# Gate groups with two tokens across the partitions, made three steps ahead, in an FNet plus PEER kernel

## The chip, the cores and the metric

The kernel runs on one core of a Trainium2 chip. The metric is the device time of one execution in microseconds. Times of one version are given as the median of several runs; the profile is one execution with the hardware profiler.

## The reference

```python
def _A_ref(x, ...):                       # FNet: real part of a 2-D Fourier transform
    a = einsum("bsd,ed->bse", x, dft_hid_re); b = einsum("bsd,ed->bse", x, dft_hid_im)
    return einsum("ts,bse->bte", dft_seq_re, a) - einsum("ts,bse->bte", dft_seq_im, b)

def _B_ref(x, w_q, k1, k2, u, v):         # PEER: 4096 experts of one neuron, S=2048, D=512, H=32, E=64
    q = einsum("nd,dhc->nhc", xf, w_q); q1, q2 = q[..., :128], q[..., 128:]
    s1 = einsum("nhd,ed->nhe", q1, k1); s2 = einsum("nhd,ed->nhe", q2, k2)
    # the two best of s1 and of s2, the two best of their four sums: expert = i1 * 64 + i2
    g = softmax(top_s)                                    # two gates for each token and head
    act = gelu(einsum("nd,nhkd->nhk", xf, u[top_e]))
    return einsum("nhk,nhk,nhkd->nd", g, act, v[top_e])

xn = layernorm(x)
return x + _A_ref(xn, ...) + _B_ref(xn, ...)
```

The Fourier matrices are inputs, and the kernel uses their symmetries, so it also checks on the chip that they have them.

## The kernel before, in words

The program has three stages. The first, to about 50 us, computes the Fourier half, with folded matrices. The second, to about 443 us, computes the scores of 16 blocks of 128 tokens for eight groups of heads, finds the best two with VectorE, and leaves for each token 64 pairs (two experts of 32 heads) of expert number and gate. The third, the expert stage, is where the change lies. (A second copy of the program for inputs without these symmetries stands behind it and is not run.)

**The expert stage, block by block.** Fourteen blocks of 128 tokens go through all 4096 experts with dense matmuls; the last two blocks (256 tokens) are done by gathering rows instead. For a block `b`:

- `u_part(b, cg)`, eight steps: products of the block's input `xb` with 4 of the 32 expert columns (48 products of 128 columns, L959), then GELU on ScalarE (L962) into `act`.
- Gates: a dense table of gates, 128 x 32 experts for each token, is itself made by matmuls. `compact` transposes a block's pairs, so that the 128 partitions hold a token's 64 pairs twice: once with the f16 high part of the gate, once with the rest. `g_mm(b, tg)` makes the table of 32 tokens: for every token a tile `L` (partition by 128: is this the expert's lower number?) and a tile `R` (partition by 32: is this its upper number?, times the gate) come from comparisons on VectorE, L983 in two halves of 16 tokens, L991 and L994, and one product of L and R gives the token's 128 x 32 gates in PSUM (L996, 32 columns). A block has four such groups. They go into two PSUM tiles `pg` of two banks in turn.
- `w_part(b, tg)`: VectorE multiplies the group's gates by the activations in place (L1007), ScalarE takes the f16 high half (L1012), VectorE subtracts it for the low half (L1015). The last subtraction frees the PSUM tile.
- `v_part(b, pv, cg)`, eight steps: 12 products of 512 columns each with `v` (L1024), accumulated; `finish` adds and stores (L1039).

**The order.** The main loop runs, for b from 0 to 13, eight steps of `v_part(b)` and then eight steps of `u_part(b + 2)`. Dictionaries say at which step a group is made (`vg`, `ug`) and at which it is used (`vw`, `uw`). Before, a group of block b + 1 was made in v steps 3 and 7 and in u steps 3 and 7, and used in v steps 0 and 4 and u steps 0 and 4. For the last block the groups 2 and 3 were made at v steps 2 and 4 and all four used at v steps 0, 2, 4, 6. Within an engine, a scheduler sets the order of instructions; every engine works through its queue in order.

**Between the steps** other work is spread. `pick` takes one piece of the gathered tokens' work for each step: `fetch` (an indirect DMA of a row of u and v into one of `BUFS` = 6 buffers `ga`), `dot` on VectorE (L1066), `gain` on ScalarE (L1076 to L1079) and an addition on GpSimd (L1084), which then issues the next fetch. `paced` takes the checks: `compare` (a slice of the Fourier matrices, L755, L761), `compare_r` (rows, L1129 to L1135), `compare_w` (the wide matrices, L1153 to L1174) and `fit`. Each loads into one of three buffers with the tag `w` through SP's queue, which also carries `xb` (L942), `zb` (a block's pairs) and `y`. `after(k, f)` puts `f` k steps later. At the end `verdict` reduces the checks with two reductions over partitions on GpSimd (L1210, L1212) and makes the `flags` (L1231) on which the program branches.

Of the kernel before, what the change touches and what calls it, by code (L numbers as in the profile page):

```python
# [36 lines left out]
def tile_fnet_peer(ctx, tc, x, ca, cb, c5, wt, wf, wr, wq, kt, ut, vn, uv, out):  # L37
# [14 lines left out]
    z_d = dram.tile([NT, P, 3 * P], F16, name="z_d")  # L52
# [503 lines left out]
    def part_b(safe, stS, stP, stE, xt, u_sb, cmp_p):  # L556
# [55 lines left out]
        z = sp.tile([P, NT, 3, 2, 2, H], F16, name="z")  # L612
# [17 lines left out]
        def routing(part, j, vals, idx, t0=0, t1=NT, ge=nc.gpsimd):  # L630
# [20 lines left out]
            elif part == 1:  # L651
# [5 lines left out]
                nc.vector.tensor_copy(zi[:, :, 2, :, 0, hs], g)  # L657
                if not safe and t1 == NT:
                    nc.gpsimd.tensor_copy(gts[:, :, :, hs], g[:, n - NS:])
                nc.vector.tensor_tensor(zi[:, :, 2, :, 1, hs], g, zi[:, :, 2, :, 0, hs], op=ALU.subtract)  # L660
            else:
# [25 lines left out]
                for l in range(2):  # L687
                    for w, v in enumerate((lc, e)):
                        ge.tensor_copy(zi[:, :, w, :, l, hs], v)
# [3 lines left out]
        def compact(b, src, pool, tag):  # L693

            cmp = pool.tile([P, 3, P, 2], F16, tag=tag, name=f"cmp{b}")
# [3 lines left out]
            nc.scalar.activation(cmp, p[:, :3 * P].rearrange("p (w n) -> p w n", w=3).unsqueeze(3)  # L699
                                 .to_broadcast([P, 3, P, 2]), AF.Copy)  # L700
            CMP[b] = cmp
# [163 lines left out]
        for j in range(NCH):  # L865
# [8 lines left out]
            for i in range(NT):  # L874
                spare, mm = scores(j, i, vals, idx)
                for f in () if safe else checks.get(j * NT + i, ()):
                    f(mm)
                for t, f in ((j * NT + i, y_rows), (j * NT + i - 10, y_store)):
                    if t in HID and not safe:
                        f(HID[t])  # L880
                if j == 1 and not safe:
                    nc.sync.dma_start(xt_d[i], xt[i].rearrange("p a k n -> p (a k n)"))
                mst = MST if j else MST0
                if j + 1 < NCH and i in mst:
                    m_stage(j + 1, wq_tile, mst[i])
                if j == 0 and i == 10 and not safe:
                    sums()
                if j + 2 < NCH and i == 9:
                    m_stage(j + 2, wq_tile, 0)
                if i in (1, 2, 4) and pend is not None:  # L890
                    routing((0, 2, None, 1)[i - 1], *pend)
                if j + 1 == NCH and i == 4:
                    for part in range(3):
                        routing(part, j, vals, idx, 0, 4, nc.vector)
                if j + 1 == NCH and i == NT - 1:
                    for b in range(2):
                        compact(b, z[:, b].rearrange("p w k t h -> p w (k t h)"), cmp_p, f"cmp{b}")
                    nc.sync.dma_start(z_d[2:4].rearrange("i p f -> p i f"),
                                      z[:, 2:4].rearrange("p i a k t h -> p i (a k t h)"))
# [8 lines left out]
        nc.sync.dma_start(z_d[4:].rearrange("i p f -> p i f"),  # L908
                          z[:, 4:].rearrange("p i a k t h -> p i (a k t h)"))
# [7 lines left out]
        RS = [lr.tile([P, 32, NC], F16, name=f"R{k}") for k in range(2)]  # L917
# [16 lines left out]
        BUFS = 6  # L934
# [10 lines left out]
        def compact_d(b):  # L945
            zb = bp.tile([P, 3, P], F16, tag="zb", name=f"zb{b}", bufs=1)
# [27 lines left out]
        def g_mm(b, tg, after=None):  # L974
            cmp = CMP[b]
            p = pg(f"g{b}_{tg}")
            def bc(w, t0, t1, n):
                return cmp[:, w, tg * TG + t0:tg * TG + t1, :].unsqueeze(2).to_broadcast([P, t1 - t0, n // 2, 2])

            for hf in range(2):  # L980
                LS.append(LS.pop(0))
                L = LS[-1]
                nc.vector.tensor_tensor(  # L983
                    L.rearrange("p t (l two) -> p t l two", two=2),
                    io_lam.rearrange("p (l two) -> p l two", two=2).unsqueeze(1).to_broadcast([P, 16, P // 2, 2]),
                    bc(0, hf * 16, hf * 16 + 16, P), op=ALU.is_equal)
                if hf == 0:
                    RS.append(RS.pop(0))
                    R = RS[-1]
                    Rv = R.rearrange("p t (c two) -> p t c two", two=2)  # L990
                    nc.vector.tensor_tensor(  # L991
                        Rv, io_c.rearrange("p (c two) -> p c two", two=2).unsqueeze(1)
                        .to_broadcast([P, TG, NC // 2, 2]), bc(1, 0, TG, NC), op=ALU.is_equal)
                    nc.vector.tensor_tensor(Rv, Rv, bc(2, 0, TG, NC), op=ALU.mult)  # L994
                for t in range(16):
                    i = nc.tensor.matmul(p[:, hf, t * NC:(t + 1) * NC], L[:, t, :], R[:, hf * 16 + t, :],  # L996
                                         start=True, stop=True)
                    if after is not None:
                        follow(i.ins, after)
# [109 lines left out]
        def compare_r(n):  # L1109
# [14 lines left out]
            def work():  # L1124
                for ri, odd, e in cls:
                    sgn = (((1, 1, 1), (-1, 1, -1)), ((-1, -1, 1), (1, -1, -1)))[ri][odd]
                    f = (-1 if ri else 1) * sgn[1] * sgn[2]
                    m = ALU.add if ri else ALU.subtract
                    nc.vector.tensor_tensor(tv[e, 1], tv[e, 1], tv[e, 0], op=ALU.subtract if sgn[0] > 0 else ALU.add)  # L1129
                    nc.vector.tensor_tensor(tv[e, 3], tv[e, 3], tv[e, 2], op=ALU.subtract if f > 0 else ALU.add)  # L1130
                    nc.vector.tensor_tensor(t[e, 0::2, 2:4], t[e, 0::2, 2:4], t[e, 0::2, 0:2], op=m)
                    if odd and ri:
                        nc.vector.tensor_copy(t[e, 2, 0:2], t[e, 0, 0:2])
                    elif odd == ri:
                        nc.vector.memset(t[e, 2, 0:2], 0.0)  # L1135
                after(2, lambda: nc.scalar.activation(tf[:, P:], tf[:, P:], AF.Abs, accum_out=chk[:, n:n + 1]))

            after(2, work)

        def compare_w(n):  # L1140
# [7 lines left out]
            if half:  # L1148
# [4 lines left out]
            nc.vector.tensor_reduce(asum[:, n:n + 1], v[0], axis=AX.X, op=ALU.add, apply_absolute_value=True)  # L1153
            nc.vector.tensor_tensor(v[1][:, even], v[1][:, even], v[0][:, even], op=op)
            nc.vector.tensor_tensor(v[1][:, odd], v[1][:, odd], v[0][:, odd], op=po)
            nc.vector.tensor_tensor(v[3][0:1], v[3][0:1], v[2][0:1], op=op)
            nc.vector.scalar_tensor_tensor(v[3][:, even], v[0][:, even], not0, v[3][:, even],  # L1157
                                           op0=ALU.mult, op1=ALU.subtract)
            nc.vector.scalar_tensor_tensor(v[3][:, odd], v[0][:, odd], not0, v[3][:, odd],  # L1159
                                           op0=ALU.mult, op1=ALU.add)  # L1160

            r = v[2][0:1]
            a, m = (slice(0, P, 2), slice(P, 256, 2)) if ri else (slice(1, P - half, 2), slice(P + 1, 256 - half, 2))
            nc.vector.tensor_tensor(r[:, m], r[:, m], r[:, a], op=op)  # L1164
            nc.vector.memset(r[:, 1 - ri:P:2], 0.0)  # L1165
            if half and not ri:
                nc.vector.memset(r[:, 255:256], 0.0)
            nc.vector.scalar_tensor_tensor(v[2], v[0], not0, v[2], op0=ALU.mult, op1=op)  # L1168
            if ri:
                nc.scalar.activation(v[0][0:1, 0:P], v[0][0:1, 0:P], AF.Abs, accum_out=chk[0:1, 69 + half:70 + half])  # L1170
            c = P - half
            nc.vector.tensor_tensor(v[0][:, P:P + c], v[0][:, P:P + c], v[0][:, 0:c], op=op)  # L1172
            if half and not ri:
                nc.vector.memset(v[0][:, 255:256], 0.0)  # L1174
            f = t.rearrange("p k e -> p (k e)")[:, P - half * ri:]
            after(2, lambda: nc.scalar.activation(f, f, AF.Abs, accum_out=chk[:, n + 1:n + 2]))
# [60 lines left out]
        units.insert(2, lambda: compare_r(64))  # L1237
# [43 lines left out]
        for tg in range(2):  # L1281
            g_mm(1, tg)
# [8 lines left out]
        for b in range(NB):  # L1291
            pv = pc(f"v{b}")
            if b + 2 < NB:
                vw, vg, uw, ug = {0: 0, 4: 1}, {3: 2, 7: 3}, {0: 2, 4: 3}, {3: 0, 7: 1}
            else:
                vw, vg = {0: 0, 2: 1, 4: 2, 6: 3}, {2: 2, 4: 3}
            for cg in range(8):
# [27 lines left out]
                elif b:  # L1325
                    pick(mm, cg % 2)
# [7 lines left out]
            for cg in range(8 if b + 2 < NB else 0):  # L1334
# [6 lines left out]
                if cg in ug:  # L1341
                    g_mm(b + 2, ug[cg], mm)
# [150 lines left out]
```

## Time and profile before

| | |
|---|---|
| median of 3 runs | 1110.06 us (1107.38 to 1111.2) |
| profiled execution, its own time | 1110.31 us |
| its span | 1108.5 us |
| TensorE busy (PE) | 1070.5 us, 97% |
| VectorE busy (DVE) | 963.9 us, 87% |
| ScalarE busy (ACT) | 717.3 us, 65% |
| GpSimd busy (POOL) | 595.4 us, 54% |
| DMA | 178 GB/s mean |

In the rows that follow, a group reads: line, engine, operation, output <- inputs, shape, count | busy us, mean ns | idle us before, and what ended it. A row of the waits reads: engine and line <- engine and line waited for: us in total, times, longest. A row of the timeline starts with its time and its length in us.

### The profile page before, as it was taken

What the parts mean: (1) busy time and instruction counts of PE and PEld (TensorE: products, weight loads), DVE (VectorE), ACT (ScalarE), POOL (GpSimd) and SP (SyncE); (2) the same over time, 40 slices, a digit from 0 to 9 for tenths busy, and PEclk for the clock granted to TensorE, in tenths of its full rate; (3) what the DMA queues carried; (4) which work ended last, traced back from release to release, by engine and by line L of the source; (5) the groups of instructions that cost most, each with busy time, mean ns of one, the idle gap of its engine ahead of it and who ended that gap; (6) DMA issues with size and microseconds to landing.
All of it is one profiled execution on the core that took longest, in us unless ns stands there. A gap on an engine that the chain in (4) does not pass through costs nothing. (4 is left out here: it accounts for less than half of the span.)

```text
span 1108.5 us, 28483 instructions
## 1 busy us (share of the span) xinstructions
PE 1070.5 (97%) x11070; PEld 696.6 (63%) x11070; DVE 963.9 (87%) x2748; ACT 717.3 (65%) x1326; POOL 595.4 (54%) x553
## 2 busy tenths in 40 slices
PE   5899999999999999999989999999999999999987
PEld 4355555454544544987675967858667696776933
DVE  6879897979999999987999798999998889998971
ACT  3566657778788767533756766668666776767650
POOL 0013537588797846211646575665575656556431
PEclk9799999999999999999999999999999999999999
DMA  8248153435445331463568667766876667666511
GB/s 326 84 168 288 39 210 99 174 130 208 152 153 197 110 123 65 152 212 92 183 189 248 193 206 244 223 220 191 242 232 214 209 204 252 222 200 200 166 29 51
DMA packets 84936, 196.78 MB, mean 178 GB/s; under 512 B 10770, under 2 KB 27559, under 8 KB 84792
## 3 DMA queue, kind: packets, MB, share of 16 engines
q1 hardware_dynamic: 63898, 123.55, 33.0%
q0 software_dynamic: 20736, 71.31, 21.7%
q8 instruction: 88, 1.44, 0.5%
q14 instruction: 56, 0.46, 0.1%
q10 hardware_dynamic: 158, 0.01, 0.0%
HBM read 177.74 MB, written 17.10 MB: 176 GB/s over the span
## 5 line engine op out<-in xcount | busy, mean ns | idle before, releaser
L799 PE MATMUL s<-m,xq 128*128 128x512 f16 x1536 | 338.9, 379 | 0.0
L959 PE MATMUL z<-xb,u 128*128 128x128 f16 x5376 | 306.4, 220 | 0.0
L959 PEld LDWEIGHTS <-u 128*128 128x128 f16 x5376 | 302.1, 98 | 0.0
L1024 PE MATMUL v<-v,act 128*128 128x512 f16 x1344 | 300.2, 382 | 1.6 <-DVE act L1015 1.6
L1084 POOL TENSOR_TENSOR ov<-ov,ga 128x512 f32<-128x512 f32 x128 | 176.9, 1382 | 206.9 <-ACT ga L1079 173.4
L799 PEld LDWEIGHTS <-xq 128*128 128x128 f16 x1536 | 148.3, 98 | 171.3 <-issue 0.2
L1024 PEld LDWEIGHTS <-act 128*128 128x128 f16 x1344 | 129.6, 98 | 153.2 <-issue 4.5
L983 DVE TENSOR_TENSOR L<-io_lam,cmp 128x2048 f16<-128x2048 f16 x112 | 154.7, 1405 | 31.2 <-PE g L996 31.1
L1050 POOL DMA_INDIRECT ga<-in_uv_dram,eix x128 | 153.4, 1198 | 48.1 <-POOL ov L1084 36.9
L807 DVE MAX8 vals<-ss 128x8 f32<-128x64 f32 x1024 | 152.5, 216 | 14.0 <-ACT ss L804 14.0
L962 ACT ACTIVATE act<-z,scl 128x512 f32<-128x512 f32 x112 | 76.1, 681 | 93.6 <-PE z L959 92.9
L811 DVE FIND_INDEX8 idx<-vals,ss 128x8 uint16<-128x256 f32 x256 | 107.1, 419 | 0.0
L804 ACT ACTIVATE ss<-s,wsc 128x512 f32<-128x512 f32 x112 | 75.5, 680 | 43.1 <-PE s L799 33.8
L1079 ACT ACTIVATE ga<-ga,za 128x512 f32<-128x512 f32 x128 | 92.3, 722 | 10.2 <-ACT za L1077 0.4
L781 ACT ACTIVATE cx<-cx 128x896 f32<-128x896 f32 x64 | 60.6, 947 | 48.7 <-DVE cx L761 36.3
L1066 DVE SCALAR_TENSOR_TENSOR ga<-ga,px 128x512 f32<-128x512 f32 x128 | 85.7, 676 | 0.2
L1012 ACT ACTIVATE act<-g 128x1024 f16<-128x1024 f32 x56 | 73.2, 1308 | 18.2 <-DVE g L1007 18.2
L1007 DVE SCALAR_TENSOR_TENSOR g<-act,scl,g 128x1024 f32<-128x1024 f32 x56 | 71.6, 1279 | 10.7 <-ACT act L962 6.6
L1015 DVE TENSOR_TENSOR act<-g,act 128x1024 f16<-128x1024 f32 x56 | 72.7, 1298 | 6.6 <-ACT act L1012 6.5
L169 POOL TENSOR_TENSOR wq<-wq,wh 128x1024 f16<-128x1024 f32 x26 | 55.5, 2136 | 24.2 <-ACT wq L166 23.7
L996 PE MATMUL g<-R,L 128*128 128x32 f16 x1792 | 53.8, 176 | 13.0 <-DVE act L1015 12.5
L996 PEld LDWEIGHTS <-L 128*128 128x128 f16 x1792 | 51.6, 96 | 21.7 <-DVE act L1015 8.7
(281 smaller groups left out, 1298.4 us busy)
## 6 DMA issues: line engine op xcount, KB each, us to landing
cx<-in_cb_dram SPq DMA_DIRECT2D x50, 448.0 KB
wq<-in_wq_dram SPq DMA_DIRECT2D x32, 512.0 KB
fit<-in_wq_dram SPq DMA_DIRECT2D x28, 512.0 KB
uv<-in_ut_dram SPq DMA_DIRECT2D x16, 512.0 KB
uv<-in_vn_dram SPq DMA_DIRECT2D x16, 512.0 KB
cx<-in_cb_dram SPq DMA_DIRECT2D x28, 224.0 KB
xq<-in_x_dram SPq DMA_DIRECT2D x8, 512.0 KB
xt_d<-xq SPq DMA_DIRECT2D x16, 256.0 KB
```

The costliest lines, as they stand in the source:

```text
L799: mm = nc.tensor.matmul(ps, xt[i][:, l, kd, :], m[:, r, kd, :], start=(n == 0), stop=(n == 3 * KD - 1))
L807: nc.vector.max(vals[:, i, w, :, h], s[:, g, :])
L811: nc.vector.max_index(idx[:, i, w].rearrange("p k h -> p (k h)"), vals[:, i, w, 0:2].rearrange("p k h -> p (k h)"), s[:, w * HC:g + 1, :]. ...
L959: mm = nc.tensor.matmul(p[:, cc * P:(cc + 1) * P], ug[:, l, c % 2, kd, :], xb[:, r, kd, :], start=(n == 0), stop=(n == 3 * KD - 1))
L962: GL[mm.ins.name] = nc.scalar.activation(act[:, cg * 4:cg * 4 + 4, :].rearrange("p c n -> p (c n)"), p, AF.Gelu_apprx_tanh, scale=zsc)
L983: nc.vector.tensor_tensor(L.rearrange("p t (l two) -> p t l two", two=2), io_lam.rearrange("p (l two) -> p l two", two=2).unsqueeze(1).to_ ...
L996: i = nc.tensor.matmul(p[:, hf, t * NC:(t + 1) * NC], L[:, t, :], R[:, hf * 16 + t, :], start=True, stop=True)
L1024: mm = nc.tensor.matmul(pv, w16[:, c, :, l], vg[:, r, c % 2, :], start=(c == 0 and k == 0), stop=(c == NC - 1 and k == 2))
L1050: nc.gpsimd.indirect_dma_start(out=t, out_offset=None, in_=uv, in_offset=bass.IndirectOffsetOnAxis(ap=eix[:, n].rearrange("p k h -> p (k h ...
L1066: nc.vector.scalar_tensor_tensor(t, t, 1.0, T["x"], op0=ALU.mult, op1=ALU.mult, accum_out=T["z", n][:, s:s + 1])
L1079: nc.scalar.activation(t, t, AF.Copy, scale=z)
L1084: T["a"] = nc.gpsimd.tensor_tensor(o, o, t, op=ALU.add)
```

## The change

1. A token's list of 64 pairs now lies in half of the partitions, and two tokens share one tile: the even token in partitions 0 to 63, the odd one in 64 to 127. One `L` tile (16 pairs of tokens) serves a group of 32 tokens. `R` becomes two tiles, for the high and the low part of the gate, each with 64 columns: 32 for the even token, 32 for the odd, with zeros (cleared once by GpSimd) where a partition belongs to the other token. Each pair of tokens gets two accumulating products of 64 columns.
2. VectorE makes, for a group, one `L`, one `one_hot`, and four parts of `R` (high and low, even and odd; 64 partitions, 512 elements each). `compact` transposes four times instead of three and copies with three ScalarE instructions instead of one.
3. Groups are made at v steps 1 and 5 (groups 1 and 2 of block b + 1), u step 1 (group 3 of block b + 1) and u step 5 (group 0 of block b + 2). Uses stay where they were; in the last block the last use moves from step 6 to 5.
4. `BUFS` is 5 instead of 6.
5. The work of `compare_r` and `compare_w` is cut into pieces of one step each, and the four `compare_w`, which were last, are spread among the first checks. No pieces of the gathered tokens' work are picked in v steps of block 12.

The diff, cut to its core:

```diff
-        RS = [lr.tile([P, 32, NC], F16, name=f"R{k}") for k in range(2)]
+        RS = [lr.tile([P, 2, 16, 2, NC], F16, name=f"R{k}") for k in range(2)]
+        one_hot = lr.tile([P, 16, NC], F16, name="one_hot")
+        for R in RS:
+            nc.gpsimd.memset(R, 0.0)
-        BUFS = 6
+        BUFS = 5
...
-            for w in range(3):
-                nc.tensor.transpose(p[:, w * P:(w + 1) * P], src[:, w], ident16)
-            nc.scalar.activation(cmp, p[:, :3 * P].rearrange("p (w n) -> p w n", w=3).unsqueeze(3)
-                                 .to_broadcast([P, 3, P, 2]), AF.Copy)
+            for w in range(4):
+                nc.tensor.transpose(p[:, w * P:(w + 1) * P], src[:, w:w + 2].rearrange("p w s -> p (w s)"), ident16)
+            for a, w0, w1, o in ((0, 0, 4, 0), (1, 0, 3, 1), (1, 3, 4, -3)):
+                r = slice(64 * a, 64 * a + 64)
+                nc.scalar.activation(cmp[r, w0 + o:w1 + o], p.rearrange("p (w n a) -> p w a n", w=4, a=2)[r, w0:w1, a]
+                                     .unsqueeze(3).to_broadcast([64, w1 - w0, 64, 2]), AF.Copy)
...
-            for hf in range(2):
-                LS.append(LS.pop(0))
-                L = LS[-1]
-                nc.vector.tensor_tensor(
-                    L.rearrange("p t (l two) -> p t l two", two=2),
-                    io_lam.rearrange("p (l two) -> p l two", two=2).unsqueeze(1).to_broadcast([P, 16, P // 2, 2]),
-                    bc(0, hf * 16, hf * 16 + 16, P), op=ALU.is_equal)
...
-                for t in range(16):
-                    i = nc.tensor.matmul(p[:, hf, t * NC:(t + 1) * NC], L[:, t, :], R[:, hf * 16 + t, :],
-                                         start=True, stop=True)
+            nc.vector.tensor_tensor(
+                two(L), io_lam.rearrange("p (l two) -> p l two", two=2).unsqueeze(1).to_broadcast([P, 16, P // 2, 2]),
+                bc(0, P), op=ALU.is_equal)
+            nc.vector.tensor_tensor(
+                two(one_hot), io_c.rearrange("p (c two) -> p c two", two=2).unsqueeze(1)
+                .to_broadcast([P, 16, NC // 2, 2]), bc(1, NC), op=ALU.is_equal)
+            for l in range(2):
+                for a in range(2):
+                    r = slice(64 * a, 64 * a + 64)
+                    nc.vector.tensor_tensor(two(R[r, l, :, a]), two(one_hot[r]), bc(2 + l, NC, r), op=ALU.mult)
+            pv = p.rearrange("p h n -> p (h n)")
+            for t in range(16):
+                for l in range(2):
+                    i = nc.tensor.matmul(pv[:, t * 64:(t + 1) * 64], L[:, t, :],
+                                         R[:, l, t].rearrange("p a c -> p (a c)"), start=l == 0, stop=l == 1)
...
-            after(2, work)
+            for k, c in enumerate(cls):
+                after(3 + k, lambda c=c: work(*c))
+            after(8, lambda: nc.scalar.activation(tf[:, P:], tf[:, P:], AF.Abs, accum_out=chk[:, n:n + 1]))
...
-            after(2, lambda: nc.scalar.activation(f, f, AF.Abs, accum_out=chk[:, n + 1:n + 2]))
+            for k, part in enumerate((first, second, third, last)):
+                after(2 + k, part)
+            after(7, lambda: nc.scalar.activation(f, f, AF.Abs, accum_out=chk[:, n + 1:n + 2]))
...
-        units.insert(2, lambda: compare_r(64))
+        for n in range(4):
+            units.insert(3 + 6 * n, units.pop())
+        units.insert(6, lambda: compare_r(64))
...
-                vw, vg, uw, ug = {0: 0, 4: 1}, {3: 2, 7: 3}, {0: 2, 4: 3}, {3: 0, 7: 1}
+                vw, vg, uw, ug = {0: 0, 4: 1}, {1: 1, 5: 2}, {0: 2, 4: 3}, {1: (1, 3), 5: (2, 0)}
+                if b + 3 == NB:
+                    ug[7] = 2, 1
             else:
-                vw, vg = {0: 0, 2: 1, 4: 2, 6: 3}, {2: 2, 4: 3}
+                vw, vg = {0: 0, 2: 1, 4: 2, 5: 3}, {2: 2, 4: 3}
...
-                elif b:
-                    pick(mm, cg % 2)
...
-                    g_mm(b + 2, ug[cg], mm)
+                    g_mm(b + ug[cg][0], ug[cg][1], mm)
```

How the change moves VectorE's queue shows at the start of the v steps of block 1, where block 2's gates are used (`g_0`, `g_1` are its first two groups, `cmp` its lists, `act` its activations, `ga` gathered rows, `cx` a check; what an instruction waits for stands in brackets). Before:

```order
L1007 SCALAR_TENSOR_TENSOR g_0_7307<-act_6973,scl,g_0_7307 128x32x32 [waits Activation_49]
L761 TENSOR_TENSOR cx_7468<-cx_7468 128x128 [waits DVE_49]
L983 TENSOR_TENSOR L_5792<-io_lam,cmp_6977 128x2048 [waits PE_49]
L1066 SCALAR_TENSOR_TENSOR ga_6_7196,za_7117<-ga_6_7196,px_7116 128x512 [waits DMASW1_49,Pool_49]
L983 TENSOR_TENSOR L_5793<-io_lam,cmp_6977 128x2048 [waits PE_49]
L1007 SCALAR_TENSOR_TENSOR g_1_7583<-act_6973,scl,g_1_7583 128x32x32
L1066 SCALAR_TENSOR_TENSOR ga_7_7255,za_7117<-ga_7_7255,px_7116 128x512 [waits DMASW2_49,Pool_49]
L1015 TENSOR_TENSOR act_6973<-g_0_7307,act_6973 128x32x32 [waits Activation_49]
```

The changed kernel at the same place:

```order
L1015 SCALAR_TENSOR_TENSOR g_0_7446<-act_6948,scl,g_0_7446 128x32x32 [waits Activation_49]
L762 TENSOR_TENSOR cx_7487<-cx_7487 128x128 [waits DVE_49]
L1074 SCALAR_TENSOR_TENSOR ga_6_7272,za_7097<-ga_6_7272,px_7096 128x512 [waits DMASW1_49,Pool_49]
L1074 SCALAR_TENSOR_TENSOR ga_7_7392,za_7097<-ga_7_7392,px_7096 128x512 [waits DMASW2_49,Pool_49]
L1023 TENSOR_TENSOR act_6948<-g_0_7446,act_6948 128x32x32 [waits Activation_49]
L1015 SCALAR_TENSOR_TENSOR g_1_7647<-act_6948,scl,g_1_7647 128x32x32 [waits PE_49]
L991 TENSOR_TENSOR L_5790<-io_lam,cmp_6952 128x2048
L1000 TENSOR_TENSOR R_5792<-one_hot,cmp_6952 64x16x32 x4
```

The two L tiles and the second multiply have left the place between the first multiply and its subtraction (L1015 before, L1023 now), and the second multiply now waits for its products.

VectorE's queue at the start of the v steps of block 12, where block 13's gates are used. Before:

```order
L1007 SCALAR_TENSOR_TENSOR g_0_16064<-act_15714,scl,g_0_16064 128x32x32 [waits Activation_49]
L1157 SCALAR_TENSOR_TENSOR cx_16377<-cx_16377,not_87 128x128 [waits DVE_49]
L1159 SCALAR_TENSOR_TENSOR cx_16377<-cx_16377,not_87 128x128
L1164 TENSOR_TENSOR cx_16377<-cx_16377 1x64
L1007 SCALAR_TENSOR_TENSOR g_1_16340<-act_15714,scl,g_1_16340 128x32x32 [waits PE_49]
L1165 MEMSET cx_16377 1x64 [waits DVE_49]
L983 TENSOR_TENSOR L_5792<-io_lam,cmp_15718 128x2048
L1168 SCALAR_TENSOR_TENSOR cx_16377<-cx_16377,not_87 128x256 [waits DVE_49]
L1066 SCALAR_TENSOR_TENSOR ga_61_16011,za_11802<-ga_61_16011,px_11801 128x512 [waits DMASW3_49,Pool_49]
L983 TENSOR_TENSOR L_5793<-io_lam,cmp_15718 128x2048
L1172 TENSOR_TENSOR cx_16377<-cx_16377 128x127 [waits Activation_49]
L1015 TENSOR_TENSOR act_15714<-g_0_16064,act_15714 128x32x32
```

The changed kernel:

```order
L1015 SCALAR_TENSOR_TENSOR g_0_16332<-act_15830,scl,g_0_16332 128x32x32 [waits Activation_49]
L1015 SCALAR_TENSOR_TENSOR g_1_16488<-act_15830,scl,g_1_16488 128x32x32 [waits PE_49]
L991 TENSOR_TENSOR L_5790<-io_lam,cmp_15834 128x2048
L1000 TENSOR_TENSOR R_5792<-one_hot,cmp_15834 64x16x32 [waits DVE_49]
L1000 TENSOR_TENSOR R_5792<-one_hot,cmp_15834 64x16x32 x3
L756 TENSOR_TENSOR cx_16529<-cx_16529 128x256 [waits DMAHW7_49,DMAHW6_49]
L756 TENSOR_TENSOR cx_16529<-cx_16529 128x512
L1023 TENSOR_TENSOR act_15830<-g_0_16332,act_15830 128x32x32 [waits Activation_49]
```

The wide check and the gathered row are gone from between the first multiply and its subtraction; a plain check in two parts, one L and the four R parts stand there.

GpSimd's queue at the end (`ov` sums the gathered rows, `y` is the last block's input to its sum, L1210 and L1230 the reductions over partitions). Before:

```order
L1084 TENSOR_TENSOR ov_11920<-ov_11920,ga_61_16011 128x512 [waits DMASW3_49,Activation_49,Pool_49]
L1084 TENSOR_TENSOR ov_11920<-ov_11920,ga_62_16120 128x512 [waits DMASW4_49,Activation_49,Pool_49]
L1033 DMA y_16611<-in_x_dram 128x512 [waits DMAHW1_49,DMAHW0_49,DVE_49]
L1084 TENSOR_TENSOR ov_11920<-ov_11920,ga_63_16233 128x512 [waits DMASW5_49,Activation_49,Pool_49]
L1210 ISA
L1210 ISA fr<-fa 128x2
```

The changed kernel:

```order
L1041 DMA y_16744<-in_x_dram 128x512 [waits DMAHW1_49,DMAHW0_49,DVE_49]
L1092 TENSOR_TENSOR ov_11982<-ov_11982,ga_61_16225 128x512 [waits DMASW3_49,Activation_49,Pool_49]
L1092 TENSOR_TENSOR ov_11982<-ov_11982,ga_62_16379 128x512 [waits DMASW4_49,Activation_49,Pool_49]
L1092 TENSOR_TENSOR ov_11982<-ov_11982,ga_63_16436 128x512 [waits DMASW5_49,Activation_49,Pool_49]
L1230 ISA
L1230 ISA fr<-fa 128x2
```

Two more additions now stand behind the transfer of y.

More of the change, by code (lines that the diff above doesn't have):

```diff
@@ L1168, in compare_w, with first @@
[L1168 to L1174, printed above, removed]
+            r = v[2][0:1]
+            def first():
+                nc.vector.tensor_reduce(asum[:, n:n + 1], v[0], axis=AX.X, op=ALU.add, apply_absolute_value=True)
+                nc.vector.tensor_tensor(v[1][:, even], v[1][:, even], v[0][:, even], op=op)
+                nc.vector.tensor_tensor(v[1][:, odd], v[1][:, odd], v[0][:, odd], op=po)
@@ L1175, in compare_w, with last @@
+            def last():
+                if ri:
+                    nc.scalar.activation(v[0][0:1, 0:P], v[0][0:1, 0:P], AF.Abs,
+                                         accum_out=chk[0:1, 69 + half:70 + half])
+                c = P - half
+                nc.vector.tensor_tensor(v[0][:, P:P + c], v[0][:, P:P + c], v[0][:, 0:c], op=op)
+                if half and not ri:
+                    nc.vector.memset(v[0][:, 255:256], 0.0)
             f = t.rearrange("p k e -> p (k e)")[:, P - half * ri:]
-            after(2, lambda: nc.scalar.activation(f, f, AF.Abs, accum_out=chk[:, n + 1:n + 2]))
+            for k, part in enumerate((first, second, third, last)):
+                after(2 + k, part)
@@ L1280, in part_b @@
                 g_mm(0, cg // 2 + 2)
[L1281 to L1282 removed]
+        g_mm(1, 0)
         last = list(range(V2, 16)) if safe else []
```

92 lines of the change are left out of this document (44 added, 48 removed).

## Prediction

> **What bounds the kernel now.** I read the page first, then TensorE's own waits in the expert stage (from 443 us on), then the clock by stretches, and last the timeline around the long waits.
>
> ```profile
> span 1108.5 us, 28483 instructions
> 443.00:1081.00 638.00, 623.90 (x8461) 471.50 (x8458) 572.40 (x859) 410.26 (x851) 343.48 (x272) 0.99 0.64 196
> ```
>
> The second row is the expert stage: length, then busy time of PE, weight load, DVE, ACT and POOL, the granted clock, and DMA. TensorE is busy for 623.9 of 638 us, VectorE for 572.4. So a microsecond of matmul added here is a microsecond of the end, and what can be won is the little that TensorE waits, and what these waits do to its clock:
>
> ```profile
> PE g L996 <- DVE act L1015: 12.5, 8, 3.9
> PE v L1024 <- DVE act L1015: 1.6, 1, 1.6
> PE g L996 <- DVE L L983: 0.3, 1, 0.3
> 556.00:578.00 22.00, 18.91 (x308) 17.15 (x306) 21.22 (x30) 10.86 (x23) 9.64 (x9) 0.92 0.64 193
> 798.00:820.00 22.00, 20.32 (x383) 19.50 (x381) 20.48 (x26) 18.29 (x39) 14.26 (x12) 0.98 0.80 238
> 820.00:842.00 22.00, 22.00 (x128) 10.27 (x127) 19.12 (x28) 12.94 (x30) 10.98 (x10) 0.94 0.71 211
> 1062.00:1084.00 22.00, 18.72 (x135) 8.90 (x135) 13.75 (x19) 9.97 (x20) 6.02 (x5) 0.92 0.14 31
> ```
>
> The waits are 14.4 us (total, times, longest). Almost all have one cause: a gate group's products need a PSUM buffer, and there are two, so group k+2 waits until VectorE has subtracted (L1015) in the buffer of group k. After three of these waits the clock falls below 1.00: 22 us times 0.08 + 0.02 + 0.06 + 0.08 is 5.3 us lost. Together **19.7 us** hang on VectorE's lateness. Two places show what it is late with:
>
> ```profile
> 559.80 0.43 DVE L1129 TENSOR_TENSOR cx_r<-cx_r 4x256 f32<-4x256 f32 x1
> 561.93 0.97 PE L996 MATMUL g<-R,L 128*128 128x32 f16 x32 [3.10 <-DVE act L1015]
> ...
> 1051.18 8.58 PE L1024 MATMUL v<-v,act 128*128 128x512 f16 x39
> 1054.83 1.29 DVE L1007 SCALAR_TENSOR_TENSOR g<-act,scl,g 128x1024 f32<-128x1024 f32 x1 [2.67 <-ACT act L962]
> 1056.03 1.24 DVE L1157 SCALAR_TENSOR_TENSOR cx<-cx,not 128x128 f32<-128x128 f32 x1
> 1062.33 1.30 DVE L1015 TENSOR_TENSOR act<-g,act 128x1024 f16<-128x1024 f32 x1
> 1063.68 0.95 PE L996 MATMUL g<-R,L 128*128 128x32 f16 x32 [3.92 <-DVE act L1015]
> ```
>
> Both times a check (rows of cx) stands in VectorE's queue ahead of the subtraction that TensorE is waiting for.
>
> **What goes.** A group is now made three steps before VectorE uses it instead of five. A step is 12 products of 512 columns (39 take 8.58 us above), about 2.7 us. Its PSUM buffer was wanted three steps after the previous use and is wanted five steps after it: 5.4 us more room. The longest wait of the steady blocks is 3.1 us, so there all should go. The checks in pieces help the same way (nothing extra is counted for it). The wait of 1.6 us before the last block goes because its last group is taken a step earlier (2.7 us). Only group 2 of block 13 keeps its place: made at step 2, its buffer used at step 0. There VectorE now has, between the first multiply and its subtraction, a second multiply, a list tile L, four R parts and two check pieces. From the rows above and below: 1.3 + 1.3 + 1.2 + 4 x 0.42 + 1.6, then 1.3 for the subtraction, 8.4 us from the start of the multiply. TensorE comes for it after 36 products at 0.22 (8.58 / 39), 7.9 us after the block begins. The multiply waits for the last GELU and began 3.65 us after the block (1051.18 to 1054.83); at best it begins with it. Ahead of that GELU stood a check and two rows in ScalarE's queue, now one row, so I take 0.4, near the lower end: 0.9 us of wait are left, and 4.2 at the upper end.
>
> VectorE's operations, by minimum, median and longest in the first two rows, by the mean in the others:
>
> ```profile
> L983 DVE TENSOR_TENSOR L<-io_lam,cmp x112: 1148/1216/2979, 449.2 to 1067.7; 128x2048 f16<-128x2048 f16 x112
> L991 DVE TENSOR_TENSOR R<-io_c,cmp x56: 666/682/2493, 452.6 to 1063.5; 128x1024 f16<-128x1024 f16 x56
> L983 DVE TENSOR_TENSOR L<-io_lam,cmp 128x2048 f16<-128x2048 f16 x112 | 154.7, 1405 | 31.2 <-PE g L996 31.1
> L991 DVE TENSOR_TENSOR R<-io_c,cmp 128x1024 f16<-128x1024 f16 x56 | 52.9, 944 | 1.1 <-ACT cmp L699 1.0
> L994 DVE TENSOR_TENSOR R<-R,cmp 128x1024 f16<-128x1024 f16 x56 | 48.8, 871 | 1.3
> L755 DVE TENSOR_TENSOR cx<-cx 128x512 f32<-128x512 f32 x27 | 25.7, 951 | 1.3 <-DMA cx<-in_cb_dram 1.3
> L755 DVE TENSOR_TENSOR cx<-cx 128x256 f32<-128x256 f32 x27 | 18.2, 675 | 0.5 <-DMA cx<-in_cb_dram 0.5
> ```
>
> By medians (1216 for 2048 elements, 682 for 1024) 512 elements take 0.42 us; by the means, which hold the delays beside GpSimd, at most what 1024 take, 0.91. A group had two L and two R operations, 4.6 us by the means; it has one L and five small ones, 1.4 + 5 x 0.42 = 3.5, at most 1.4 + 5 x 0.91 = 6.0. Below the bound where VectorE fills the stage (rivals), none of it reaches TensorE. One L instead of two also ends most of the 31.1 us in which VectorE itself stood still until TensorE had read an L tile; I count nothing for it.
>
> Against the small operations the Trainium skill speaks, in "VectorE: DVE Perf Modes", section "Two Vector instructions with no wait between them": an instruction whose operands start at another group of 32 partitions than the last ones is held until all earlier ones are done, and the four R parts change between partition 0 and 64. The 0.43 us of L1129 above, a row check's part that starts at another partition than its neighbours, would contain that, but the trace doesn't separate it. By the page the sum would stay, and VectorE's load would rise by what neighbours overlap.
>
> **What it adds.** Products now have 64 columns, still 32 in a group.
>
> ```profile
> 621.07 0.95 PE L996 MATMUL g<-R,L 128*128 128x32 f16 x32
> 621.88 6.30 PE L959 MATMUL z<-xb,u 128*128 128x128 f16 x110
> 88.19 0.22 PE L147 MATMUL m<-sums,wh 128*128 128x64 f16 x2
> ...
> 88.89 0.81 PE L799 MATMUL s<-m,xq 128*128 128x512 f16 x3
> L959 PE MATMUL z<-xb,u 128*128 128x128 f16 x5376 | 306.4, 220 | 0.0
> ```
>
> Of 32 columns, 32 products take 0.81 us from start to start, 25.3 ns each. Of 64 columns, the 24 products of L147 in f16, which also accumulate in place behind 128x128 weights, take 88.19 to 88.89: 29.2 ns. The difference, 3.9 ns times 1792 products, is **6.9 us**. The bounds are 25.3 ns (nothing) and the 57 ns of 128 columns (306.4 / 5376, 57 us more); the same shape in the same precision is the nearest row by far. A fourth transpose of each of 14 lists costs 57 ns: 0.8 us. Sum added: 7.7 us.
>
> **What is moved or hidden.** The rows for this part:
>
> ```profile
> 586.81 0.33 SPq L942 DMA_DIRECT2D xb<-xt_d  x1
> 610.35 1.84 PE L959 MATMUL z<-xb,u 128*128 128x128 f16 x30
> L1066 DVE SCALAR_TENSOR_TENSOR ga<-ga,px x128: 660/675/693, 518.8 to 1075.1; 128x512 f32<-128x512 f32 x128
> ga<-in_uv_dram,eix POOLq DMA_INDIRECT x128, 5.1
> ```
>
> Three copies by ScalarE for a list instead of one come several steps before VectorE wants them; ScalarE is busy for 410 of 638 us, and late copies would delay VectorE alone. Two clearings of R stand on GpSimd ahead of a copy of gates that waits for VectorE's last lists, so they are done before these. At the first group the 0.3 us stays, since VectorE's operations before it become shorter as their number grows. Five row buffers still leave four rows, some 17 us (128 rows from 518.8 to 1075.1 us), for a gather that lands in a median of 5.1; if late, VectorE would stand. The four wide checks and the row check hold one of three load buffers for seven or eight steps instead of two to four, and behind such loads the blocks' inputs queue on SP. An input goes out 23.5 us before its first product, so a delay of five steps, 14 us, stays covered; uncovered, TensorE would wait for the remainder.
>
> Block 12 picks no rows now, so three rows remain for the last block, and on GpSimd they stand behind the load of its y:
>
> ```profile
> 1079.46 0.75 DVE L1039 SCALAR_TENSOR_TENSOR y<-v,scl,y 128x512 f32<-128x512 f32 x1 [3.67 <-PE v L1024]
> 1085.41 0.90 POOL L1033 DMA_DIRECT2D y<-in_x_dram  x1 [6.71 <-DMA y<-y_d]
> 1086.02 1.58 POOL L1084 TENSOR_TENSOR ov<-ov,ga 128x512 f32<-128x512 f32 x1
> 1093.54 0.41 POOL L1210 PARTITION_ALL_REDUCE fr<-fa  x1 [5.94 <-issue]
> 1096.11 0.15 DVE L1231 TENSOR_TENSOR flags<-flag,flag 1x1 int32<-1x1 int32 x1
> 1101.96 0.75 DVE L1039 SCALAR_TENSOR_TENSOR y<-v,scl,y 128x512 f32<-128x512 f32 x1 [5.71 <-PE v L1024]
> ```
>
> The flags came 5.7 us before the last product. Now, counted from the last block's start (1081.46 to 1101.96, 20.5 us before its end): 6.9 us to the end of issuing that y transfer (1079.46 to 1086.31), 4.7 at most for three additions at 1.58, 5.9 of the gap before the reduction, 2.7 for reduction and flags: 20.2. It just fits. What slips costs its full length; I put 0.5 us (bounds 0 and 3).
>
> **The sum**, against the profiled execution's 1110.3 us (span 1108.5 and 1.8 around it; the median of the three runs is 1110.06, so 0.3%, about what a measurement can tell from no change, is 3.3 us): 19.7 goes; 7.7 comes; of waits remain 0.3 at the first group, 0.9 at block 13, 0.7 elsewhere (a guess: a quarter of one long wait), and of the clock's loss 0.6 (a third of one fall); 0.5 at the end. 1110.3 - 19.7 + 7.7 + 3.0 = **1101.3**.
>
> **The rivals.**
> (a) VectorE stays late: block 13 waits 4.2 us, half of the other waits (5) move to where the buffers are now wanted, and two clock falls of 1.8 us remain. With the first group's 0.3 that is 13.1 instead of 2.5: 1101.3 + 10.6 = 1111.9 at worst, half of it 1106.6. For it speaks VectorE's 90% in the stage and the 4.2 us above; against it 5.4 us of added room. Chance 0.18, centred on 1107.
> (b) Slower: VectorE becomes the bound through its five short operations. It has 572.4 us of work here, 256.4 of them gates (154.7 + 52.9 + 48.8); 316 others leave 312 of a stage of about 628, 5.6 us a group, so (5.6 - 1.4) / 5 = 0.84 us is the point. At 0.91 VectorE needs 334 + 316 = 650, 22 us too much: 1123. For it: the means of 0.87 to 0.94 beside GpSimd; against: medians of 0.68 for twice the size. Chance 0.10.
> (c) Wider products cost nothing: the short products are bound by a floor, not by columns. Then 6.9 us less: 1094.4. L147's 29.2 against 25.3 speaks against it. Chance 0.05. The table in "TensorE: Matmul & The Clock Gate", section "Back-to-back issue gap", of the Trainium skill says so, with one figure of about 60 cycles for 1 to 64 columns; the formula beside it, N/2.4 + 2.5 ns, gives 29.2 as this trace does.
>
> **How the numbers follow.** The forecast has 0.67 (1098 to 1105: waits left between 0.3 and 4.2, the end between 0 and 3). Range 1097 to 1108.5: it leaves out (b), (c) and the upper part of (a). Faster by over 0.3% (below 1106.7): 0.67 + 0.05 + half of (a), 0.81 less 0.03 for the unforeseen: 0.78. Same: 0.09 of (a) and 0.01 beside: 0.10. Slower: 0.12.
>
> **What would show it.** Right: TensorE's waits for L1015's successor fall from 14.1 to under 5 us, with at most one fall of the clock; the gate products take about 29 ns from start to start; VectorE's R parts have a median near 0.42 us. Wrong: products at 40 ns or more, R parts of 0.8, waits for xb, or flags after the last product.

## The result: the waits moved from the gate groups to y, and nothing was won

The changed kernel took 1112.4 us (median of 20 runs) beside 1109.46 us for the kernel before: ratio 1.0023, interval 1.0012 to 1.0034. The forecast of 1101.3 us and its range up to 1108.5 were wrong. That the time lies near the worst end of rival (a), 1111.9, is luck: what that rival was made of did not come.

The profile of the changed kernel, the same views as before the change: the span, the expert stage (length, busy time of PE, weight load, DVE, ACT, POOL, granted clock, DMA), TensorE's waits (total, times, longest), and, with the columns of the stage's row, three blocks from their first v product to the next block's.

```profile
span 1111.2 us, 28664 instructions
443.00:1081.00 638.00, 629.96 (x8472) 482.51 (x8470) 559.33 (x964) 413.67 (x870) 331.81 (x272) 0.99 0.64 196
PE z L963 <- DVE y L1047: 7.3, 2, 4.2
PE v L1032 <- DVE y L1047: 0.8, 1, 0.8
PE g L1004 <- DVE act L1023: 0.8, 1, 0.8
630.09:682.81 52.72, 48.52 (x615) 37.10 (x613) 51.32 (x78) 32.99 (x73) 31.37 (x25) 0.94 0.64 197
682.81:728.93 46.12, 46.12 (x616) 34.78 (x614) 37.49 (x61) 32.94 (x72) 28.03 (x23) 1.00 0.69 219
821.16:873.33 52.17, 49.10 (x616) 37.69 (x613) 48.93 (x79) 32.24 (x69) 29.14 (x25) 0.93 0.70 215
```

The waits for the subtraction (now L1023) fell from 14.1 us to 0.8, as forecast, and VectorE is less busy than before (559.3 against 572.4 us). But TensorE's z now waits twice for y, 7.3 us, which it never did before. A block without such a wait takes 46.12 us and keeps the full clock; the two with it take 52.72 and 52.17, with clocks of 0.94 and 0.93. That is 6.60 + 6.05 = 12.65 us: 7.3 of waits, and 5.4 more in which the products ran at the lower clock. Without it the profiled run of 1113.1 us would have been 1100.5. So the forecast failed by one wait that is not in its sum.

What y is: `finish` (L1047) multiplies the block's sum v, which lies in PSUM, and writes y; only then is v's buffer free. The z of a u step 2 or 5 takes a buffer of the same pair (tag `pc`, two buffers, L69), and while the gathered token's x (`px`) holds the other one, z of step 2 must have v's. The first of the two places, in order of time:

```profile
652.89 5.52 PE L963 MATMUL z<-xb,u 128*128 128x128 f16 x96
654.88 1.80 DVE L991 TENSOR_TENSOR L<-io_lam,cmp 128x2048 f16<-128x2048 f16 x1
657.21 4.77 DVE L1000 TENSOR_TENSOR R<-one_hot,cmp 64x512 f16<-64x512 f16 x4
657.53 1.30 POOL L1092 TENSOR_TENSOR ov<-ov,ga 128x512 f32<-128x512 f32 x1
658.25 1.10 PE L1004 MATMUL g<-R,L 128*128 128x64 f16 x32
660.42 1.27 POOL L1092 TENSOR_TENSOR ov<-ov,ga 128x512 f32<-128x512 f32 x1
662.75 0.74 DVE L1047 SCALAR_TENSOR_TENSOR y<-v,scl,y 128x512 f32<-128x512 f32 x1
663.55 4.74 PE L963 MATMUL z<-xb,u 128*128 128x128 f16 x43 [4.20 <-DVE y L1047]
```

v was complete at 652.9 us. VectorE reached y at 662.75, 9.9 us later. Until 654.88 it was still at a subtraction and a multiply of the gates; then one L tile and four R parts, 1.80 + 4.77 us, stand ahead of y, and with them a gathered row and three pieces of a check, together 1.3. The L tile and the parts are the list of block 5's first group (`cmp5` holds that block's pairs; v and y are block 3's), whose products come only in u step 5, three steps after the z that waits. VectorE's order there, cut:

```
1106 L991 TENSOR_TENSOR L0_5789<-io_lam_72,cmp5_9385 128x2048
1107 L1074 SCALAR_TENSOR_TENSOR ga0_32_9327,za0_7097<-ga0_32_9327,px0_7096 128x512
1108 L1000 TENSOR_TENSOR R0_5791<-one_hot_5793,cmp5_9385 64x16x32 x4
...
1112 L1047 SCALAR_TENSOR_TENSOR y3_9395<-v3_9240,scl_101,y3_9395 128x512
```

Four parts undisturbed take 1.71 us (at 836.77 us of the same trace); here they took 4.77, with two additions of GpSimd beside them.

### The profile page after: what moved, and what is told of

Read it like the earlier page. It is cut to its first block, busy times and chain, and to the rows that moved or that the text cites. A ratio compares the mean times of both kernels' runs of the same rounds, so it can differ in the third digit from the quotient of the medians.

```text
span 1111.2 us, 28664 instructions
## 1 busy us (share of the span) xinstructions
PE 1075.6 (97%) x11084; PEld 707.3 (64%) x11084; DVE 951.9 (86%) x2858; ACT 723.5 (65%) x1354; POOL 584.8 (53%) x548
## 4 chain that ended last, share of the span: by engine, by line
PE 78%; DVE 13%; issue 3%; DMA 2%; ACT 2%; POOL 0%; SPq 0%; DVEq 0%; POOLq 0%; ACTq 0%
PE s L800 29%; PE z L963 21%; PE v L1032 19%; PE g L1004 3%; DVE R L1000 2%; PE m L147 2%; PE p L371 2%; DVE L L991 1%; DVE g L1015 1%; DVE ga L1074 1%; DVE act L1023 1%; DVE cx L756 1%; DVE ft L348 1%; DMA wq<-in_wq_dram 0%; PE xp L431 0%
## 5 line engine op out<-in xcount | busy, mean ns | idle before, releaser
L963 PE MATMUL z<-xb,u 128*128 128x128 f16 x5376 | 311.9, 221 | 7.3 <-DVE y L1047 7.3
L963 PEld LDWEIGHTS <-u 128*128 128x128 f16 x5376 | 306.9, 99 | 10.3 <-issue 7.5
L1058 POOL DMA_INDIRECT ga<-in_uv_dram,eix x128 | 143.2, 1119 | 47.9 <-POOL ov L1092 35.7
L1000 DVE TENSOR_TENSOR R<-one_hot,cmp 64x512 f16<-64x512 f16 x224 | 142.0, 634 | 8.8 <-PE g L1004 6.1
L1023 DVE TENSOR_TENSOR act<-g,act 128x1024 f16<-128x1024 f32 x56 | 73.2, 1307 | 32.8 <-ACT act L1020 28.7
L1015 DVE SCALAR_TENSOR_TENSOR g<-act,scl,g 128x1024 f32<-128x1024 f32 x56 | 71.5, 1280 | 7.3 <-PE g L1004 5.7
L991 DVE TENSOR_TENSOR L<-io_lam,cmp 128x2048 f16<-128x2048 f16 x56 | 77.1, 1376 | 0.1
L1004 PEld LDWEIGHTS <-L 128*128 128x128 f16 x1792 | 58.6, 98 | 7.2 <-DVE act L1023 1.3
```

What stands on the lines that cost most here:

```text
L963: mm = nc.tensor.matmul(p[:, cc * P:(cc + 1) * P], ug[:, l, c % 2, kd, :], xb[:, r, kd, :], start=(n == 0), stop=(n == 3 * KD - 1))
L991: nc.vector.tensor_tensor(two(L), io_lam.rearrange("p (l two) -> p l two", two=2).unsqueeze(1).to_broadcast([P, 16, P // 2, 2]), bc(0, P), ...
L1000: nc.vector.tensor_tensor(two(R[r, l, :, a]), two(one_hot[r]), bc(2 + l, NC, r), op=ALU.mult)
L1004: i = nc.tensor.matmul(pv[:, t * 64:(t + 1) * 64], L[:, t, :], R[:, l, t].rearrange("p a c -> p (a c)"), start=l == 0, stop=l == 1)
L1058: nc.gpsimd.indirect_dma_start(out=t, out_offset=None, in_=uv, in_offset=bass.IndirectOffsetOnAxis(ap=eix[:, n].rearrange("p k h -> p (k h ...
```

## Experiments

**Theory A**: the list that the order puts ahead of y is what costs; the rest of the sum holds. **Theory B**: VectorE is late with its many short operations, and a wait that is taken away comes back elsewhere.

**Another PSUM buffer for z (e1).** No engine's order changes.

```
-p = (pc if cg in (... if b == 0 else (2, 5)) else pb)(f"z{b}_{cg}")
+p = (pc if cg in (... if b == 0 else (4, 6)) else pb)(f"z{b}_{cg}")
```

> In the changed kernel two blocks of 46.1 us took 52.7 and 52.2 us, 12.7 us too much: in both TensorE's step 2 (z) waited for y's operation on v (4.2 and 3.1 us), since z takes the PSUM buffer that v leaves, and the clock fell after it. Here z takes that buffer at steps 4 and 6 instead of 2 and 5, two steps (5.4 us) later; the order on every engine stays as it is. Theory A (the wait for y's buffer is what the prediction missed, the rest of its sum holds): the two waits and their falls go, 12.7 us less than the changed kernel, 1099 to 1102 us. Theory B (VectorE is late with its many short operations, and any next wait takes the place of this one): waits for L1023, L1015 or the lists appear at the gate groups, and the time stays above 1106 us.

Measured: 1104.69 us beside 1110.04, ratio 0.996 (0.9942 to 0.9978). Both waits for y are gone, but TensorE waits in two other places (its waits, then ScalarE and TensorE at the longer one):

```profile
PE v L1032 <- ACT act L966: 2.9, 1, 2.9
PE z L963 <- ACT act L966: 1.7, 1, 1.7
860.19 1.06 ACT L1203 ACTIVATE fit<-fit 128x1024 f32<-128x1024 f32 x1 [4.97 <-DMA fit<-in_wq_dram]
864.19 0.67 ACT L966 ACTIVATE act<-z,scl 128x512 f32<-128x512 f32 x1
864.91 2.33 PE L1032 MATMUL v<-v,act 128*128 128x512 f16 x9 [2.86 <-ACT act L966]
```

With z of steps 4 and 6 in the pair, z of step 6 waits once for ScalarE's GELU of step 4 (1.7 us), and the next block's v once for the GELU of step 6 (2.9 us). At the longer wait the GELU is late because ScalarE had stood 4.97 us for a load. Part of the gain is given back, by the experiment's own edit, so the time, 1104.69 us, lies between what the theories said. That the two waits for y fell away without one for a list or a subtraction in their place speaks for A.

**The list behind y (e2).** The PSUM buffers stay; for group 0 the L tile and the R parts follow y.

```
+i = T["fin"] = nc.vector.scalar_tensor_tensor(y, pv, osc, y, ...)
...
+if "fin" in T and tg == 0:
+    follow(i.ins, T["fin"])      # after L and after each part of R
```

> The list of the next block's group 0 (L and its four R parts, 3.9 to 6.6 us of VectorE ahead of y, with products only three steps later) is put behind y's operation in VectorE's order; the PSUM buffers stay as they are. Theory A: y is done some 4 us earlier, both waits of step 2 go, 1099 to 1102 us, as with another buffer. Theory B: the list is now late for its own products, or another wait appears, and the time stays above 1106 us.

Measured: 1102.94 us beside 1110.04, ratio 0.9927 (0.9907 to 0.9946), where the changed kernel has 1.0023: 0.96%, or 10.7 us. VectorE and TensorE at the same place, and the longest wait that is left:

```profile
657.01 0.74 DVE L1051 SCALAR_TENSOR_TENSOR y<-v,scl,y 128x512 f32<-128x512 f32 x1
657.67 2.45 DVE L991 TENSOR_TENSOR L<-io_lam,cmp 128x2048 f16<-128x2048 f16 x1
660.04 2.94 DVE L1002 TENSOR_TENSOR R<-one_hot,cmp 64x512 f16<-64x512 f16 x3
659.04 1.10 PE L1008 MATMUL g<-R,L 128*128 128x64 f16 x32
659.98 10.21 PE L963 MATMUL z<-xb,u 128*128 128x128 f16 x180
PE v L1036 <- DVE cx L764: 1.9, 1, 1.9
```

y is done before z of step 2 wants its buffer, TensorE goes on without a gap, and of waits one of 1.9 us and two of 0.8 are left. Theory A holds: the time is 0.9 us above the 1099 to 1102 expected, 1.6 above the prediction's 1101.3 and below B's 1106. B's waits for the lists did not come; the wait of 1.9 us is one for VectorE, put down to a check.

**GpSimd's additions cut to 8 columns (e6).** The order on VectorE and TensorE is the changed kernel's, list ahead of y.

```
-T["a"] = nc.gpsimd.tensor_tensor(o, o, t, op=ALU.add)
+T["a"] = nc.gpsimd.tensor_tensor(o[:, :8], o[:, :8], t[:, :8], op=ALU.add)
```

> The changed kernel with GpSimd's additions on 8 columns instead of 512 (the rest of each gathered row is left out of the sums); the order on VectorE and TensorE stays. In the changed kernel 17 of 224 R parts that lay beside an addition and an indirect DMA took 1.85 us instead of 0.42, and three of them stand ahead of each late y. If the length of these parts comes from the additions, their mean falls from 0.63 to about 0.43 us, L's from 1.38 to 1.22; the waits for y fall from 4.2 and 3.1 to at most 1.2 us, and the time to 1099 to 1103 us. If the parts are long for another reason (their change of partitions, TensorE reading R), the mean stays near 0.6 and the time near 1112.

Measured: 1099.52 us beside 1112.32, ratio 0.988 (0.9861 to 0.99), within the 1099 to 1103 expected. The R parts of the changed kernel (minimum, median, longest; then busy, mean):

```profile
L1000 DVE TENSOR_TENSOR R<-one_hot,cmp x224: 401/422/2185, 453.7 to 1064.7; 64x512 f16<-64x512 f16 x112
L1000 DVE TENSOR_TENSOR R<-one_hot,cmp 64x512 f16<-64x512 f16 x224 | 142.0, 634 | 8.8 <-PE g L1004 6.1
```

The same of this one, the wait for y that is left, and VectorE and TensorE at the place of the first late y:

```profile
L1000 DVE TENSOR_TENSOR R<-one_hot,cmp x224: 386/421/475, 453.0 to 1051.5; 64x512 f16<-64x512 f16 x112
L1000 DVE TENSOR_TENSOR R<-one_hot,cmp 64x512 f16<-64x512 f16 x224 | 93.8, 419 | 10.4 <-PE g L1004 7.8
PE v L1032 <- DVE y L1047: 0.8, 1, 0.8
651.35 1.21 DVE L991 TENSOR_TENSOR L<-io_lam,cmp 128x2048 f16<-128x2048 f16 x1
653.09 1.71 DVE L1000 TENSOR_TENSOR R<-one_hot,cmp 64x512 f16<-64x512 f16 x4
653.49 5.52 PE L963 MATMUL z<-xb,u 128*128 128x128 f16 x96
655.57 0.75 DVE L1047 SCALAR_TENSOR_TENSOR y<-v,scl,y 128x512 f32<-128x512 f32 x1
```

No part is longer than 0.475 us now, and no wait for y at step 2 is left although the list still stands ahead of it. So it takes both: the list ahead of y, and the additions that hold VectorE up. They do so in two ways that this run does not part. The list is shorter (3.5 us from the start of L to the end of the parts, 7.1 in the changed kernel). And VectorE comes to it earlier, 2.1 us before v is complete instead of 2.0 after, since it is held up less everywhere (475.4 us of work in the stage instead of 559.3, and the parts make 48 of that difference). Together y begins 2.1 us after v, not 9.9. So Theory B's first half, that VectorE is late, has a share in the wait.

That the additions stretch the parts, and not the indirect DMA that GpSimd also issues, shows in the changed kernel's trace as well: all 43 parts over 0.48 us overlap an addition, and 42 of them end 0.28 to 0.30 us after one does; of the 167 that overlap none, the longest takes 0.45. The Trainium skill, "Trainium Architecture — The Big Picture", section "What this means for kernel authors", calls the port pair that VectorE and GpSimd share an exclusive lock, "not a bandwidth split". Parts of 0.42 us that take up to 2.19 and end with an addition of 1.3, and none above 0.475 beside additions of 8 columns, agree with that.

**The two halves apart (e3, e4, e5).** Lists and places of the groups, each with all else of the change (checks in pieces, five row buffers, no picks in block 12). e3 has the lists and products of before at the new places; its edit in words:

```
-R = (L tile; one_hot; four parts of R; 32 products of 64 columns)
+R = (two L tiles; compare and multiply of 1024; 32 products of 32 columns)
```

> The lists and products of before (two L tiles and two operations of 1024 elements for R, products of 32 columns) with all else of the change: groups three steps ahead, five row buffers, checks in pieces. The products cost 7.2 us less (1792 x 4.0 ns) and the fourth transposes go. In the order y stands behind one L tile and the compare of R, about 2 us, instead of 4 to 6. Theory A: y is early enough, TensorE hardly waits, some 1093 us. If the groups' new places alone bring the waits for y, or VectorE stands for free L tiles, waits of 5 us and more remain and it is 1098 to 1104.

e4 has the new lists at the old places, those of the last block too (cut to the main line):

```
-vw, vg, uw, ug = {0: 0, 4: 1}, {1: 1, 5: 2}, {0: 2, 4: 3}, {1: (1, 3), 5: (2, 0)}
+vw, vg, uw, ug = {0: 0, 4: 1}, {3: 2, 7: 3}, {0: 2, 4: 3}, {3: (2, 0), 7: (2, 1)}
```

> The new lists and products of 64 columns with the groups at the places of before (made five steps ahead); checks in pieces and five row buffers as in the change. The prediction's account of before: the waits for the subtraction, 14 us and 5 us of clock, come from the places, so they stay, and 8 us of products come on top: 1115 to 1120 us. If the checks in pieces had removed most of those waits: 1102 to 1106 us.

e5 has both as before, so that only the checks in pieces, the row buffers and the picks remain of the change (the diff is e3's and e4's together):

> The kernel before with only the checks in pieces, five row buffers and no picks in block 12; lists, products and the groups' places as before. With e4 it gives what the lists alone cost. If the lists cost at the old places just their products and transposes (7.2 + 0.8 us), this run is 8 us under e4's 1120.6: 1112 to 1113 us, and the pieces have brought nothing. If the pieces took away half of the 14 us of waits, as the prediction allowed for, it is near 1100, and the lists cost 20.

Measured, as ratios to the kernel before:

| | old lists | new lists |
|---|---|---|
| old places | e5: 0.9932 (0.9915 to 0.9949) | e4: 1.0089 (1.0071 to 1.0108) |
| new places | e3: 0.9903 (0.9883 to 0.9923) | the change: 1.0023 (1.0012 to 1.0034) |

TensorE's longest waits in e3, then in e4, then in e5:

```profile
PE v L1024 <- DVE act L1015: 3.1, 2, 2.5
PE g L996 <- DVE act L1015: 1.3, 1, 1.3
PE z L959 <- DVE y L1039: 1.1, 1, 1.1
```

```profile
PE g L1004 <- DVE act L1023: 14.8, 11, 5.3
PE v L1032 <- DVE y L1047: 0.8, 1, 0.8
```

```profile
PE g L996 <- DVE act L1015: 9.2, 6, 3.3
PE v L1024 <- DVE y L1039: 0.8, 1, 0.8
```

The checks in pieces, with the five row buffers and without the picks, took 0.68% (7.5 us); which of the three did it was not tried. The gate products' waits for the subtraction fell from 12.5 to 9.2 us. That is between the two expectations, which had said nothing or some 10. On top of it the new places gave 0.3% with the old lists, which is hardly clear of the noise (the intervals overlap), and 0.7% with the new ones.

e3's 1099.67 us is above its main expectation (1093) and within the other: some waits remained, among them one for y. e4's 1120.59 us is just above its main expectation (1115 to 1120). The new lists cost 1.6% at the old places (17 us) and 1.2% at the new (13 us), not the 7.7 of the sum. The products' part is there in both; the rest is waits and what the clock loses after them, in e4 for the subtraction, in the change for y.

**What the parts add up to (e7).** The old lists at the new places, y ahead of the next block's R, and the last block's v in the other pair of PSUM buffers.

```
+if "fin" in T and tg == 0:
+    follow(i.ins, T["fin"])      # after the compare of R
...
-pv = pc(f"v{b}")
+pv = (pb if b + 1 == NB else pc)(f"v{b}")
```

> The best of the parts: the lists and products of before, groups three steps ahead, y's operation ahead of the next block's R, and the last block's v in the PSUM buffer pair that z has left, so that it needn't wait for y of block 12. Against the run with the old lists at the new places (waits of 6.7 us): its waits for y of 1.1 and 0.8 us go, the rest stays: 1097 to 1099 us. If y behind R's compare cost nothing, the time stays at 1099.7.

Measured: 1094.59 us beside 1112.32, ratio 0.9835 (0.9814 to 0.9857), 18 us less than the kernel before and the fastest here; better than the 1097 to 1099 expected. Its stage and its waits for the subtraction:

```profile
443.00:1081.00 638.00, 635.65 (x8544) 477.50 (x8543) 573.13 (x872) 409.74 (x852) 354.82 (x277) 1.00 0.67 198
PE g L998 <- DVE act L1017: 1.3, 1, 1.3
PE v L1026 <- DVE act L1017: 0.6, 1, 0.6
```

TensorE is busy for 635.7 of 638 us, with VectorE as busy as before the change (573.1). Beside the waits for y, which are gone, e3's two waits of v for the subtraction (3.1 us) became one of 0.6; why those shrank was not tried.

## Why the prediction was wrong

- **The waits for the subtraction** go: right, 14.1 to 0.8 us; at block 13's group 2 0.9 was forecast and 0.77 came. But the reason was only half right. For the checks in pieces "nothing extra is counted", and they won 7.5 us together with the row buffers and the picks; the places, to which the sum gives all, added 3 to 7.
- **Products**: right. In e2 the 32 products of 64 columns take 659.04 to 659.98, 29.4 ns each, against 29.2 forecast. An undisturbed block takes 46.12 us with the new lists and 45.53 with the old ones in e3 (491.25 to 536.78), 0.59 more, or 8.3 in 14 blocks, where the sum had 7.7 for products and transposes.
- **The list operations**: the size was right. A group costs 1376 + 582 + 4 x 634 ns = 4.5 us of VectorE, within 3.5 to 6.0 and like the 4.6 before (the rows below and e6's). What the prediction left open, the changed kernel's trace answers: an R part never begins before the part ahead of it has ended (152 pairs), while the operation after a one_hot mostly begins some 0.08 us before that one's end (45 of 56).

```profile
L991 DVE TENSOR_TENSOR L<-io_lam,cmp 128x2048 f16<-128x2048 f16 x56 | 77.1, 1376 | 0.1
L994 DVE TENSOR_TENSOR one_hot<-io_c,cmp 128x512 f16<-128x512 f16 x56 | 32.6, 582 | 11.5 <-ACT cmp L700 10.4
```

- **The step that failed**: "Below the bound where VectorE fills the stage, none of it reaches TensorE." The bound is one of mean load. The prediction followed the moved steps past the queues of SP, GpSimd and ScalarE, but not past y in VectorE's own order, and did not ask which PSUM buffer waits for y. Its one missing line is 12.65 us, and 1101.3 + 12.65 = 1114 is the measured time within 2 us. Rival (a) had the direction, VectorE late where the buffers are now wanted, but looked for it at the gate groups' buffers; there block 13 waits 0.77 us, not its 4.2.
- **The other omission of that kind** is small. The wait of 1.6 us before the last block was to go with the subtraction, but 0.84 of it stays: the last block's v takes the buffer of block 12's v, so it waits for y as well. Before, y's operation (from 1079.46, in the prediction's rows) stood ahead of the subtraction in the same wait, which is put down to what ended last:

```profile
1080.13 1.27 DVE L1015 TENSOR_TENSOR act<-g,act 128x1024 f16<-128x1024 f32 x1
1081.46 2.77 PE L1024 MATMUL v<-v,act 128*128 128x512 f16 x12 [1.60 <-DVE act L1015]
```

e4 and e5, with the groups at the old places, have the same 0.8, so the groups' places do not make it; in e7, with the other pair of buffers, it is gone.

- **The end**: 0.5 us was put in for a late verdict. The verdict is in time, with some 2 us to spare where the sum of 20.2 us left 0.3: the last y waited 2.14 us for its products, with the flags set before it.

```profile
1101.90 0.15 DVE L1251 TENSOR_TENSOR flags<-flag,flag 1x1 int32<-1x1 int32 x1
1104.19 0.75 DVE L1047 SCALAR_TENSOR_TENSOR y<-v,scl,y 128x512 f32<-128x512 f32 x1 [2.14 <-PE v L1032]
```

- **Rival (b)** did not come (R parts 0.63 us on the mean, 0.84 was its point), nor (c).

## What to carry to other kernels

When a step is made at another time, list everything that it now stands ahead of in the queue of the engine that makes it, and for each the buffer that it frees and who waits for that. Here the order put work that was needed late, but could start early, ahead of a short operation that was needed at once; making the list follow y was worth some 10 us. A mean load of VectorE below 100% said little, where one run of operations could take nearly three times its length (4.77 us instead of 1.71).

## What was not expected of the hardware

Whether TensorE's clock falls after a wait does not follow from the wait's length alone. In e5 a wait of 2.92 us was followed by a granted clock of 0.92 over 22 us, and one of 3.28 us by 1.00 (the two waits in the timeline, then the two stretches):

```profile
621.99 1.00 PE L996 MATMUL g<-R,L 128*128 128x32 f16 x32 [2.92 <-DVE act L1015]
821.80 0.95 PE L996 MATMUL g<-R,L 128*128 128x32 f16 x32 [3.28 <-DVE act L1015]
618.00:640.00 22.00, 19.09 (x296) 16.61 (x294) 19.15 (x30) 14.63 (x30) 9.97 (x8) 0.92 0.60 169
818.00:840.00 22.00, 18.72 (x154) 9.63 (x152) 21.96 (x37) 13.44 (x29) 13.72 (x11) 1.00 0.82 245
```

And short operations in place of long ones were no gain beside GpSimd: by the median a part of 512 elements takes 0.42 us, by the mean 0.63, since each can be held by an addition, and a group's list costs VectorE 4.5 us where it cost 4.6.
